# Start addresses of the float32r operand tiles: 32 and 224 bytes past a multiple of 256, or on it

## The chip, the core and the metric

The kernel runs on one core of one Trainium2 chip. The metric is the time of one execution on the device in microseconds (us). Before the change it is 1198.25 us, the median of three runs (1197.19 to 1199.11 us).

## The reference

All inputs are float32. Three layers follow one another, over 4 x 576 = 2304 tokens of width 8 heads x 64 = 512:

```
a      = softmax of phi over the tokens, per memory slot      # 32 slots a head
k_m    = a^T k ;  v_m = a^T v                                 # 32 x 64 per head
x      = softmax(q k_m^T / 8) v_m                             # 2304 x 512
h      = x @ w_in ;  g = h * clip(h + 3, 0, 6) / 6            # 512 -> 2048
x      = g @ w_out                                            # 2048 -> 512
p      = probs / (sum(probs) + 1e-9)                          # 4 experts
out    = sum over e of p[:, e] * (relu(x @ w1[e]) @ w2[e])    # 512 -> 1024 -> 512
```

## The kernel before

A large product is made of three float32r matmuls (`PASSES`): each operand is kept as a rounded part and the rest, (hi, lo) side by side in one tile, and hi x hi, hi x lo and lo x hi are summed in PSUM. The two attention products with short sums, the transposes and `u_mm` stay in plain float32; they are few.

First stage: attention and the first FFN, over four blocks of 512 of the 2048 hidden columns. `u_mm` folds a block of `w_in` into `v_m` and gives tile `u`; `g1` (line 528) multiplies a 128-column slice of `u` (stationary) with a half of the batch's attention tile `attnT` (moving, 288 tokens); line 535 to 539 and the casts at lines 287 and 290 make `g`; `g2` (line 555) multiplies slices of `w_out` (stationary) with `g` (moving, 288 wide). The order of this stage is worked out by a planner while the program is built, from fixed costs, and is then fixed.

Second stage: the four experts, 8 chunks `c` of 512 hidden columns. Tokens go in blocks `t` of 512, 512, 512, 512 and 256. `m1` (line 681) runs 12 matmuls for each of four slices `i`: stationary a 128 x 128 slice of a weight tile `w`, moving `x2[t]`, as wide as the block. ScalarE and VectorE make the hidden tile `h` (lines 685 and 686). `m2` (line 700) runs, two items later, 12 matmuls (6 for the short block): stationary a slice of `h`, moving a weight tile `w`, 512 wide. So an item is 12 matmuls of line 681 and 12 (6) of line 700, taking turns. VectorE adds each finished 128 x 512 result into `oacc` (line 711).

Memory: pools lie on two stacks in SBUF, one growing up (`side="left"`), one growing down (`side="right"`). Addresses below are bytes in a partition. The left stack begins at 16512, behind 16384 bytes of DMA descriptors and four constants at 32 bytes each. Pool `const` takes 512 (`ident`), 32 (`three`, padded), 288 (`pr`) and 96 bytes (`psm`, padded), so the next pool begins at 17440 = 68 x 256 + 32. Pools `rawp`, `w_lo`, `acc_lo` and, in the second stage, `w_hi`, `acc_hi`, `x_lo` follow in multiples of 256: all weight tiles `w` (float32r) and `x2[0]` lie 32 bytes past a multiple of 256. The right stack begins at 229344 = 895 x 256 + 224 and also goes in multiples of 256 down to `u`, `attnT`, `g`, and in the second stage `h` and `x2[1]` to `x2[4]`: all of these lie 224 bytes past a multiple of 256.

Slices keep this, except halves of 288 float32 = 1152 bytes = 4.5 x 256: the second half of a batch's tokens in `attnT` and the lo part of `g` begin 128 bytes further, at 96 past a multiple of 256.

| matmul | moving, bytes past a multiple of 256 | stationary |
|---|---|---|
| `g1`, line 528, 768 times, 288 wide | 224 (u = 0) or 96 (u = 1) | 224 |
| `g2`, line 555, 1536 times, 288 wide | 224 (hi, two of three) or 96 (lo) | 32 |
| `m1`, line 681, 384 times, t = 0 | 32 | 32 |
| `m1`, 1152 times, t = 1 to 3 | 224 | 32 |
| `m1`, 384 times, t = 4, 256 wide | 224 | 32 |
| `m2`, line 700, 1728 times, 512 wide | 32 | 224 |

Of the kernel before, what the change touches and what calls it, by code (L numbers as in the profile page):

```python
# [9 lines left out]
F32 = mybir.dt.float32  # L10
# [13 lines left out]
P = 128  # L24
# [101 lines left out]
def body(ctx: ExitStack, tc: tile.TileContext, phiT, kv, qT, w_in, w_out, w1, w2, dp, out):  # L126
    nc = tc.nc
    ctx.enter_context(tc.manual_schedule())

    const = ctx.enter_context(tc.tile_pool(name="const", bufs=1, side="left"))  # L130
    rawp = ctx.enter_context(tc.tile_pool(name="rawp", bufs=4, side="left"))
    w_lo = ctx.enter_context(tc.tile_pool(name="w_lo", bufs=1, side="left"))
    acc_lo = ctx.enter_context(tc.tile_pool(name="acc_lo", bufs=1, side="left"))
    ps_acc = ctx.enter_context(tc.tile_pool(name="ps_acc", bufs=1, space=PSUM))
    ps_w = ctx.enter_context(tc.tile_pool(name="ps_w", bufs=4, space=PSUM))
    ph1 = ExitStack()
    keep = ph1.enter_context(tc.tile_pool(name="keep", bufs=1, side="right"))
    wip = ph1.enter_context(tc.tile_pool(name="wip", bufs=8, side="right"))
# [618 lines left out]
```

## Time and profile before

| | |
|---|---|
| median of three runs | 1198.25 us |
| the profiled execution | 1200.89 us |
| its span in the profile | 1198.9 us |
| busy: TensorE / VectorE / ScalarE | 1175.5 / 550.9 / 329.8 us |
| granted TensorE clock, mean | 0.992 of 2.4 GHz |

The profile is of one execution. "PE" is TensorE's matmuls, "PEld" its weight loads, which run beside them; DVE is VectorE and ACT is ScalarE. The profiler gives a matmul a length that overlaps the next one's, since matmuls are pipelined. So the cost of a matmul in a stream is not its "mean ns" but the step from its start to the start of the next one. In a timeline, which merges neighbours of one line into a row, that is the start of the next row less the start of this row, divided by this row's count. Starts are given to 0.01 us.

### The profile page before, as it was taken

How to read it: one execution, taken by the hardware profiler on the slowest of the kernel's cores; microseconds unless marked ns; L12 is line 12 of the kernel's file. 1: busy time of each engine (PE TensorE's matmuls, PEld its weight loads, DVE VectorE, ACT ScalarE, POOL GpSimd, SP SyncE). 2: the span in 40 equal slices, each digit the busy share in tenths (PEclk: the TensorE clock that was granted, in tenths of full speed). 3: DMA queues.
4: the chain of work that ended last, by engine and by line, in shares of the span. 5: the costliest groups of instructions: out<-in, count | busy, mean ns of one | idle time of the engine just before them, and what ended most of it. 6: DMA issues, size and time to landing. Idle time of an engine off the chain costs nothing.

```text
span 1198.9 us, 16170 instructions
## 1 busy us (share of the span) xinstructions
PE 1175.5 (98%) x6776; PEld 1009.0 (84%) x6776; DVE 550.9 (46%) x1117; ACT 329.8 (28%) x713; POOL 1.2 (0%) x8
## 2 busy tenths in 40 slices
PE   4899999999999999999999999999999999999998
PEld 3699999999999888888888888888888888888887
DVE  7988898995665352323232323232323232323222
ACT  2665655454544231111111011011112111101100
POOL 0000000000000000000000000000000000000000
PEclk8899999999999999999999999999999999999999
DMA  9852131210100000000010010000001001000011
GB/s 358 264 172 79 39 103 37 71 54 19 36 1 1 9 18 9 27 27 18 9 36 27 1 36 27 9 27 27 18 10 36 27 1 36 27 9 1 36 55 69
DMA packets 20408, 55.86 MB, mean 47 GB/s; under 512 B 2416, under 2 KB 2416, under 8 KB 19824
## 3 DMA queue, kind: packets, MB, share of 16 engines
q1 hardware_dynamic: 20336, 54.83, 13.8%
q8 instruction: 53, 0.87, 0.3%
q14 instruction: 19, 0.16, 0.0%
HBM read 50.11 MB, written 4.72 MB: 46 GB/s over the span
## 4 chain that ended last, share of the span: by engine, by line
PE 97%; DVE 1%; ACT 1%; DMA 0%; issue 0%; ACTq 0%
PE ph L681 33%; PE pacc L700 33%; PE pacc L555 17%; PE ph L528 8%; PE psc L376 2%; PE pu L512 1%; PE pk L350 1%; PE pa L333 0%; PE pe L421 0%; DMA raw<-in_w_in 0%; ACT phi L317 0%; ACT a L340 0%; DVE oacc L711 0%; DVE w L221 0%; DVE mx L308 0%
## 5 line engine op out<-in xcount | busy, mean ns | idle before, releaser
L681 PE MATMUL ph<-x,w 128*128 128x512 f32 (+1 forms) x1920 | 426.8, 371 | 0.0
L700 PE MATMUL pacc<-w,h 128*128 128x512 f32 x1728 | 425.1, 394 | 0.0
L681 PEld LDWEIGHTS ph<-x,w 128*128 128x128 f32 x1920 | 337.9, 188 | 69.8
L700 PEld LDWEIGHTS pacc<-w,h 128*128 128x128 f32 x1728 | 322.7, 188 | 72.3
L686 DVE SCALAR_TENSOR_TENSOR h<-ph,h 128x512 fp32r<-128x512 f32 (+1 forms) x160 | 102.2, 639 | 557.2 <-ACT h L685 557.2
L685 ACT ACTIVATE h<-ph 128x512 fp32r<-128x512 f32 (+1 forms) x160 | 88.9, 555 | 673.8 <-PE ph L681 673.8
L555 PE MATMUL pacc<-g,w 128*128 128x288 f32 x1536 | 221.4, 296 | 1.7 <-DVE w L193 1.0
L555 PEld LDWEIGHTS pacc<-g,w 128*128 128x128 f32 x1536 | 208.2, 188 | 10.3 <-issue 6.7
L528 PE MATMUL ph<-attnT,u 128*128 128x288 f32 x768 | 116.8, 296 | 0.4 <-ACT vmT L365 0.4
L528 PEld LDWEIGHTS ph<-attnT,u 128*128 128x128 f32 x768 | 106.3, 188 | 5.0 <-issue 1.0
L711 DVE SCALAR_TENSOR_TENSOR oacc<-pacc,pr,oacc 128x512 f32<-128x512 f32 x126 | 86.3, 744 | 2.6 <-PE pacc L700 2.6
L287 ACT CAST g<-t 128x288 fp32r<-128x288 f32 x128 | 55.4, 434 | 89.5 <-PE pacc L555 76.8
L535 ACT ACTIVATE t<-ph,three 128x288 f32<-128x288 f32 x128 | 62.6, 501 | 32.0 <-DVE g L290 22.5
L290 DVE TENSOR_TENSOR g<-t,g 128x288 fp32r<-128x288 f32 x128 | 56.6, 454 | 23.7 <-ACT g L287 23.3
L539 DVE SCALAR_TENSOR_TENSOR t<-t,ph 128x288 f32<-128x288 f32 x128 | 56.6, 450 | 10.1 <-ACT t L535 10.1
L567 DVE TENSOR_TENSOR acc<-pacc,acc 128x288 f32<-128x288 f32 x96 | 39.7, 457 | 31.1 <-PE pacc L555 31.1
L193 DVE TENSOR_TENSOR w<-raw,w 128x512 fp32r<-128x512 f32 x64 | 43.6, 682 | 0.1
L189 ACT CAST w<-raw 128x512 fp32r<-128x512 f32 x64 | 39.1, 613 | 0.0
L376 PEld LDWEIGHTS psc<-kmT,q 128*128 128x128 f32 (+1 forms) x160 | 20.7, 213 | 3.5 <-issue 3.0
L376 PE MATMUL psc<-kmT,q 128*128 128x64 f32 (+1 forms) x160 | 21.7, 298 | 1.5 <-DVE mx L311 1.5
L333 PE MATMUL pa<-ident,phi 128*128 128x128 f32 (+1 forms) x40 | 8.4, 353 | 14.8 <-ACT phi L317 14.8
L290 DVE TENSOR_TENSOR u<-pu,u 128x512 fp32r<-128x512 f32 x32 | 21.4, 681 | 1.5 <-ACT u L287 1.5
(59 smaller groups left out, 364.2 us busy)
## 6 DMA issues: line engine op xcount, KB each, us to landing
raw<-in_w SPq DMA_DIRECT2D x64, 256.0 KB, 2.7
raw<-in_w_in SPq DMA_DIRECT2D x16, 512.0 KB, 4.0
kv<-in_kv SPq DMA_DIRECT2D x16, 512.0 KB, 7.5
raw<-in_w_out SPq DMA_DIRECT2D x16, 512.0 KB, 3.3
q<-in_qT SPq DMA_DIRECT2D x4, 1152.0 KB, 5.4
out_y<-oacc SPq DMA_DIRECT2D x18, 256.0 KB, 2.1
phi<-in_phiT SPq DMA_DIRECT2D x4, 576.0 KB, 7.9
kv<-in_kv SPq DMA_DIRECT2D x4, 256.0 KB, 9.6
```

Of the source, the lines that this page charges most:

```text
L287: nc.scalar.copy(hi, src)
L290: nc.vector.tensor_tensor(out=lo, in0=src, in1=hi.bitcast(F32), op=ALU.subtract)
L376: nc.tensor.matmul(ps[:n, j].rearrange("p (o g) m -> p g o m", o=2)[:, hp], st["q", b][:, hp, s0:s0 + n], kmT[b % 2][:, hp].rearrange("p ( ...
L528: nc.tensor.matmul(ps, uts[c, b][:, x, hq, i * P:(i + 1) * P], attnT[b][:, y, hq, u * UN:(u + 1) * UN], start=(k == 0), stop=(k == 5))
L535: nc.scalar.activation(t, st["ph", n], AF.Relu, bias=three, scale=1.0)
L539: nc.vector.scalar_tensor_tensor(out=t, in0=t, scalar=6.0, in1=st.pop(("ph", n)), op0=ALU.min, op1=ALU.mult)
L555: nc.tensor.matmul(pacc[j][:, 0:UN], w[:, x, j * P:(j + 1) * P], g[:, y], start=(i == 0 and k == 0), stop=(i == NI - 1 and k == 2))
L681: nc.tensor.matmul(ps[:, 0:T], wsp[c, kt][:, x, i * P:(i + 1) * P], x2[t][:, y, kt], start=(k == 0), stop=(k == 11))
L685: nc.scalar.activation(h[:, 0, 0:T], ps[:, 0:T], AF.Relu)
L686: nc.vector.scalar_tensor_tensor(out=h[:, 1, 0:T], in0=ps[:, 0:T], scalar=0.0, in1=h[:, 0, 0:T].bitcast(F32), op0=ALU.max, op1=ALU.subtract)
L700: nc.tensor.matmul(ps, h[:, x, j * P:(j + 1) * P], wsp[c, 4 + i][:, y], start=(i == 0 and k == 0), stop=(i == NI - 1 and k == 2))
L711: nc.vector.scalar_tensor_tensor(out=o, in0=ps, scalar=sc, in1=o, op0=ALU.mult, op1=ALU.add)
```

## The change

A tile of 56 float32 (224 bytes) a partition is put at the beginning of the left stack and another at the beginning of the right stack. Nothing reads or writes them. Everything on the left stack moves up by 224 bytes and everything on the right moves down by 224 bytes. The weight tiles and `x2[0]` come to 32 + 224 = 256, and `u`, `attnT`, `g`, `h` and `x2[1]` to `x2[4]` to 224 - 224 = 0: all begin on a multiple of 256. The 1152-byte halves (`attnT` for u = 1, the lo part of `g`) begin at 128 past one. No instruction is added, removed or moved.

```diff
     const = ctx.enter_context(tc.tile_pool(name="const", bufs=1, side="left"))
+
+    const.tile([P, 56], F32, name="edge")
     rawp = ctx.enter_context(tc.tile_pool(name="rawp", bufs=4, side="left"))
...
     ps_w = ctx.enter_context(tc.tile_pool(name="ps_w", bufs=4, space=PSUM))
+    edge = ctx.enter_context(tc.tile_pool(name="edge", bufs=1, side="right"))
+    edge.tile([P, 56], F32, name="edge_r")
     ph1 = ExitStack()
```

## Rows read from the trace of the kernel before

**Rows 1.** The page, parts 1 and 2: busy times, and the granted clock in 40 slices

```profile
PE 1175.5 (98%) x6776; PEld 1009.0 (84%) x6776; DVE 550.9 (46%) x1117; ACT 329.8 (28%) x713; POOL 1.2 (0%) x8
...
PEclk8899999999999999999999999999999999999999
```

**Rows 2.** The page, part 4: the chain that ended last, by line

```profile
PE ph L681 33%; PE pacc L700 33%; PE pacc L555 17%; PE ph L528 8%; PE psc L376 2%; PE pu L512 1%; PE pk L350 1%; PE pa L333 0%; PE pe L421 0%; DMA raw<-in_w_in 0%; ACT phi L317 0%; ACT a L340 0%; DVE oacc L711 0%; DVE w L221 0%; DVE mx L308 0%
```

**Rows 3.** Busy time by stretch; PE, PEld, DVE, ACT, POOL, granted clock, DMA share, GB/s

```profile
40.00:60.00 20.00, 18.02 (x238) 14.77 (x231) 19.15 (x48) 15.21 (x39) 0.00 (x0) 0.99 0.86 279
60.00:345.00 285.00, 284.90 (x2322) 269.68 (x2322) 232.89 (x539) 154.71 (x348) 0.00 (x0) 1.00 0.20 64
345.00:1190.00 845.00, 845.00 (x4006) 702.58 (x4005) 266.93 (x463) 145.16 (x296) 0.00 (x0) 1.00 0.07 22
```

**Rows 4.** Groups by line, who waits; count, busy us, mean ns, idle before and releaser

```profile
L681 PEld LDWEIGHTS ph<-x,w 128*128 128x128 f32 x1920 | 337.9, 188 | 69.8
...
L686 DVE SCALAR_TENSOR_TENSOR h<-ph,h 128x512 fp32r<-128x512 f32 (+1 forms) x160 | 102.2, 639 | 557.2 <-ACT h L685 557.2
L685 ACT ACTIVATE h<-ph 128x512 fp32r<-128x512 f32 (+1 forms) x160 | 88.9, 555 | 673.8 <-PE ph L681 673.8
```

**Rows 5.** Groups by line and shape, matmuls from 400 to 1100 us

```profile
L700 PE MATMUL pacc<-w,h 128*128 128x512 f32 x1511 | 372.0, 394 | 0.0
L681 PE MATMUL ph<-x,w 128*128 128x512 f32 x1345 | 329.7, 393 | 0.0
L681 PE MATMUL ph<-x,w 128*128 128x256 f32 x336 | 44.2, 281 | 0.0
```

**Rows 6.** Timeline of PE, end of block t=4, begin of t=0: start, length, line, count

```profile
489.05 1.58 PE L681 MATMUL ph<-x,w 128*128 128x256 f32 x12
490.47 1.56 PE L700 MATMUL pacc<-w,h 128*128 128x512 f32 x6
491.86 2.88 PE L681 MATMUL ph<-x,w 128*128 128x512 f32 x12
494.58 1.54 PE L700 MATMUL pacc<-w,h 128*128 128x512 f32 x6
```

**Rows 7.** Timeline of PE, end of block t=0, then t=1, in the same chunk

```profile
505.51 2.88 PE L681 MATMUL ph<-x,w 128*128 128x512 f32 x12
508.23 2.91 PE L700 MATMUL pacc<-w,h 128*128 128x512 f32 x12
510.98 2.96 PE L681 MATMUL ph<-x,w 128*128 128x512 f32 x12
513.78 2.96 PE L700 MATMUL pacc<-w,h 128*128 128x512 f32 x12
516.58 2.96 PE L681 MATMUL ph<-x,w 128*128 128x512 f32 x12
519.38 2.93 PE L700 MATMUL pacc<-w,h 128*128 128x512 f32 x12
522.14 2.96 PE L681 MATMUL ph<-x,w 128*128 128x512 f32 x12
```

**Rows 8.** Timeline of PE in the first stage, 288 wide

```profile
223.11 1.75 PE L528 MATMUL ph<-attnT,u 128*128 128x288 f32 x12
224.70 1.75 PE L555 MATMUL pacc<-g,w 128*128 128x288 f32 x12
...
231.45 0.95 PE L528 MATMUL ph<-attnT,u 128*128 128x288 f32 x6
232.24 0.95 PE L555 MATMUL pacc<-g,w 128*128 128x288 f32 x6
...
237.79 0.97 PE L528 MATMUL ph<-attnT,u 128*128 128x288 f32 x6
238.60 3.34 PE L555 MATMUL pacc<-g,w 128*128 128x288 f32 x24
241.78 0.97 PE L528 MATMUL ph<-attnT,u 128*128 128x288 f32 x6
```

## The prediction

> **What bounds the kernel now.** I read the page's busy times first: TensorE's matmuls take 1175.5 us of the 1198.9 us span, and the granted clock is at its upper level of 2.4 GHz but for the first two slices [rows 1]. The chain of waits says the same from the other end: lines 681, 700, 555 and 528, the four float32r products, hold 33 + 33 + 17 + 8 = 91% of the path [rows 2]. By stretches TensorE has no gap that counts from 60 us on: 284.9 of 285 us and 845 of 845 us [rows 3]. VectorE and ScalarE wait for it in the second stage, ScalarE 674 us ahead of line 685 and VectorE 557 us ahead of line 686, and the weight loads of line 681 have 69.8 us of idle time of their own [rows 4]. So the time is a number of matmuls times the step from one start to the next. No instruction comes or goes; only that step can change, by the operands' addresses. What the trace can say of that is whether matmuls of one shape at different addresses have different steps now.
>
> **They do.** Line 681 runs the same 12 matmuls, 512 wide, from the same weight tiles for token blocks 0 to 3. For block 0, where both operands lie 32 past a multiple of 256, a run of 12 takes 505.51 to 508.23, so 2.72 us or 226.7 ns each; the run at 491.86 to 494.58 takes the same 2.72 us [rows 6, 7]. For block 1, with `x2` at 224, the runs at 510.98 and 516.58 take 2.80 us, 233.3 ns each [rows 7]. That is 6.6 ns or 2.9% between two runs a few microseconds apart, same line, same width, same clock. Line 700, moving operand at 32 and stationary at 224, lies between: 2.75, 2.80 and 2.76 us, so 229.2, 233.3 and 230.0 ns [rows 7].
>
> **The change, part by part.** The two added tiles are written by nobody, so they cost no instruction. DMAs keep their sizes, their order and their queue, and the order on every engine is fixed when the program is built. Nothing waits anew. What moves is start addresses, and the terms are the four products.
>
> 512 wide (line 700, 1728 times; line 681 for four blocks, 1536 times; 3264 in all). From 400 to 1100 us TensorE is never idle, and the stretch holds 336 matmuls 256 wide and 1511 + 1345 = 2856 that are 512 wide [rows 5]. A 256-wide one takes (490.47 - 489.05) / 12 = 118.3 ns [rows 6], together 39.8 us, which leaves 660.2 us / 2856 = 231.2 ns for a 512-wide one. After the change both operands of all of them begin on a multiple of 256. The nearest row for that is block 0 of line 681, both operands at the same place past a multiple of 256, at 226.7 ns. I take this value: 3264 x 4.5 ns = 14.7 us less. The ends: 512 columns at the granted 2.4 GHz are 213.3 ns, and if the step fell to that, it would be 3264 x 17.9 = 58.4 us less; if all went to the dearest step that the rows show for this width, 233.3 ns, 3264 x 2.1 = 6.9 us more.
>
> 256 wide (line 681, block 4, 384 times). Now 118.3 ns with operands at 224 and 32. No row shows this width aligned. If the aligned step went with the width it would be 226.7 / 2 = 113.3 ns, 1.9 us less; if it got worse as the dearest 288-wide row does against its usual one (135.0 against 132.5), 0.8 us more. A fixed part of the step may well not shrink, so I take half of the gain, 0.9 us less.
>
> 288 wide (lines 528 and 555, 2304 times). The runs are 132.5 ns (223.11 to 224.70, and 238.60 to 241.78), 131.7 (231.45) and 135.0 (237.79) [rows 8]. Line 528 has its operands at 224 and 224 or at 96 and 224, line 555 at 224 or 96 and 32. After it half of line 528 and two thirds of line 555 are at 0 and 0, the rest at 128 and 0, since a half of 1152 bytes is no multiple of 256. The steps here don't fall apart by address as those of line 681 do, which speaks for a small effect. Ends: 226.7 x 288 / 512 = 127.5 ns would be 2304 x 5.0 = 11.5 us less; 135.0 for all would be 2304 x 2.5 = 5.8 us more. I take 131.5, by the row at 131.7 which is nearest: 2.3 us less. Some of these matmuls lie in the first 60 us, where TensorE also waits for others; a part of 2.3 us doesn't matter there.
>
> Everything else (float32 products, transposes, VectorE, ScalarE, the DMAs) also moves by 224 bytes. Their float32 matmuls have 2 + 1 + 1 = 4% of the chain [rows 2], 48 us, and a 1% change of all of them would be 0.5 us to either side; I take nothing. That TensorE stays the bound is safe: a second stage that is 15 us shorter still leaves VectorE 267 us of work in some 830 [rows 3].
>
> Sum: 14.7 + 0.9 + 2.3 = 17.9 us less. The profiled execution took 1200.9 us, so it would come to 1183.0. That execution lies 2.6 us over the median of 1198.25, so the median comes to 1180.4; I say 1180.
>
> A rule that speaks against the change: the Trainium skill, "SBUF — State Buffer", section "Specifications (TRN2)", gives SBUF lines of 16 bytes and a penalty for each step to a new line, and its section "Operand start alignment" asks of a start address no more than a multiple of the element size (and says that its runs timed nothing). Since 32 and 224 are multiples of 16 as 256 is, by that rule no step would change and the time would stay at 1198. The rows differ from it: 226.7 against 233.3 ns for two starts that both are multiples of 16 [rows 7].
>
> **The rivals.** *No effect.* Block 0 differs from blocks 1 to 3 in more than the address: in it ScalarE and VectorE also convert weights, and `x2[0]` was made in the first stage. If something of that kind sets the step, the time stays at 1198. Against it: more work beside TensorE should not make its matmuls faster, and line 700 is at 229.2 ns in the same block, so it isn't the moment. This is also what the skill's rule on lines of 16 bytes gives. Chance 0.07.
>
> *The moving operand alone decides.* Line 700's moving operand lies at 32 already, as that of the fast runs of line 681 does, and it still needs 229 to 233 ns. If it does so for a reason of its own (it alternates between the hi and lo part of one weight tile, and loads the same stationary slice twice), only blocks 1 to 3 of line 681 gain: 1152 x 6.6 = 7.6 us, 1190.6. Against it: its stationary operand at 224 is the one thing that the table of addresses gives for it. Chance 0.10.
>
> *32 is not the floor.* Nothing in the trace begins at 0. If a start at 32 costs the 512-wide step as much over one at 0 as 224 costs over 32, 6.6 ns, the step is 220.1 and 3264 x 6.6 = 21.5 us more go, to 1159; the narrower ones could add to that. For it: 226.7 is still 13.4 ns over 512 columns at 2.4 GHz. Against it: the 256-wide step is 11.6 ns over its 106.7, so most of that seems a fixed part. Chance 0.12. The Trainium skill, "TensorE: Matmul & The Clock Gate", section "Back-to-back issue gap", gives width / 2.4 + 2.5 ns for an isolated step, 215.8 at 512; an estimate by that page for all three widths is 3264 x 15.4 + 384 x 9.1 + 2304 x 10.0 = 77 us less, 1121. No row here comes near it.
>
> *Slower.* With every operand on a multiple of 256, a weight load and the moving read beside it begin on the same place within 256 bytes. If that is where they get in each other's way, the 512-wide step goes to 233.3 and, with the 128-byte halves, the 288-wide one to 135.0: 6.9 + 5.8 = 12.7 us more, 1211. It decides once the common place costs more than 4.5 ns a matmul against what the rows at 32 show. Against it: block 0 of line 681 has just that, both at 32, and is the fastest. Chance 0.04.
>
> **How the numbers follow.** My forecast has 0.67. All of it, the moving-operand rival and the rival of a lower floor are faster by over 0.2% (2.4 us, about what a measurement here can tell from no change): 0.67 + 0.10 + 0.12 = 0.89; within it 0.07; slower 0.04. The range goes from 1157 (the lower floor for 512 wide, which leaves out its further half, 0.06) to 1196 (which holds the moving-operand case and leaves out no effect and slower, 0.11): 0.17 left out. Within it, the 288-wide bounds alone move the forecast from 1171 to 1189.
>
> **What would show it.** In the timeline after, runs of 12 of line 681 last 2.72 us in all blocks 0 to 3, and those of line 700 too; the second stage is some 15 us shorter and the first some 2. If line 700 stays at 2.75 to 2.80 the moving operand alone decides; if block 0 also gets shorter than 2.72, 32 was not the floor; if blocks 1 to 3 stay at 2.80, the address was not the reason. A run of line 528 over 0.81 us for 6 would show that the 128-byte halves cost. The forecast fails if no row of line 681 gets faster, or if one that was at 226.7 gets slower.

## The result, and the profile after

The changed kernel takes 1186.38 us, the median of four runs (1184.58 to 1189.32), against 1197.72 us before: ratio 0.991, 95% interval 0.9883 to 0.9936. It is 11 us faster; 1180 was forecast. In a second series of runs, further down, the ratio was 0.9866 (0.9846 to 0.9887). Part of that spread is the clock that an execution was granted: at a mean clock of 0.993 the executions on record took 1200.5 to 1201.5 us before (four) and 1187.0 to 1187.7 after (three), at 0.997 they took 1196.7 to 1198.7 (three) and 1182.2 to 1183.1 (two). At an equal clock the change is thus worth some 14 us.

Part 5 of the page before, and then parts 1 and 5 of the page after (line 681 is now 685, line 700 is 704, 528 is 532 and 555 is 559):

```profile
L681 PE MATMUL ph<-x,w 128*128 128x512 f32 (+1 forms) x1920 | 426.8, 371 | 0.0
L700 PE MATMUL pacc<-w,h 128*128 128x512 f32 x1728 | 425.1, 394 | 0.0
```

```profile
PE 1162.9 (98%) x6776; PEld 1010.3 (85%) x6776; DVE 550.9 (46%) x1117; ACT 329.7 (28%) x713; POOL 1.2 (0%) x8
...
L685 PE MATMUL ph<-x,w 128*128 128x512 f32 (+1 forms) x1920 | 419.7, 368 | 0.0
L704 PE MATMUL pacc<-w,h 128*128 128x512 f32 x1728 | 418.3, 390 | 0.0
...
L532 PE MATMUL ph<-attnT,u 128*128 128x288 f32 x768 | 116.8, 296 | 0.4 <-ACT vmT L369 0.4
```

Counts and the other engines' busy times are as in [rows 1]. The two groups of the second stage are shorter; line 528 had 116.8 us before, as line 532 has now. The timeline of TensorE around the end of block 4 and into blocks 0 and 1, which answers to [rows 6, 7]; columns: start, length, line, count:

```profile
478.46 1.60 PE L685 MATMUL ph<-x,w 128*128 128x256 f32 x12
479.89 2.91 PE L704 MATMUL pacc<-w,h 128*128 128x512 f32 x12
482.64 1.60 PE L685 MATMUL ph<-x,w 128*128 128x256 f32 x12
...
506.06 2.88 PE L685 MATMUL ph<-x,w 128*128 128x512 f32 x12
508.78 2.88 PE L704 MATMUL pacc<-w,h 128*128 128x512 f32 x12
511.50 2.88 PE L685 MATMUL ph<-x,w 128*128 128x512 f32 x12
514.22 2.88 PE L704 MATMUL pacc<-w,h 128*128 128x512 f32 x12
516.94 2.88 PE L685 MATMUL ph<-x,w 128*128 128x512 f32 x12
```

In blocks 0 and 1 every run of 12 that is 512 wide now starts 2.72 us ahead of the next one, 226.7 ns a matmul, on line 685 and on line 704; behind a 256-wide run line 704 takes 2.75 (479.89 to 482.64). Before it was 2.72 in block 0, 2.80 in block 1 and 2.75 to 2.80 on line 700 [rows 7]. The 256-wide run got longer: 1.43 us, 119 ns, where it was 1.42 [rows 6]. The first stage, answering to [rows 8]:

```profile
225.05 1.76 PE L532 MATMUL ph<-attnT,u 128*128 128x288 f32 x12
226.64 1.75 PE L559 MATMUL pacc<-g,w 128*128 128x288 f32 x12
```

12 matmuls of line 532 in 1.59 us are 132.5 ns, the same as before to the 0.01 us of the rows.

The trace keeps the starts to the nanosecond, so the steps can be summed over all matmuls of a kind. Before and after, in us: line 681 with 512 columns 355.8 and 348.2; line 700 399.2 and 392.4; line 681 with 256 columns 45.2 and 45.8; line 528 104.3 and 104.5; line 555 208.2 and 208.6. Together that is 13.2 us less, of which the span shows 11.6. The other 1.6 us went in the first 60 us: the matmul that began at 60.05 us before begins 1.7 us later after the change. That stretch by busy time, before and then after (columns as in [rows 3]):

```profile
0.00:60.00 60.00, 40.45 (x428) 32.71 (x429) 49.17 (x114) 29.58 (x70) 1.21 (x8) 0.86 0.88 311
```

```profile
0.00:60.00 60.00, 39.44 (x403) 31.64 (x403) 49.13 (x114) 29.31 (x68) 1.20 (x8) 0.83 0.86 308
```

TensorE got 0.83 of its clock there against 0.86, and was 25 matmuls behind at 60 us. The clock varies from run to run of one kernel: the four runs of the changed kernel had mean clocks of 0.991, 0.993, 0.996 and 0.995 with times of 1189.3, 1187.0, 1185.8 and 1184.6 us.

### The profile page after: what moved, and what is told of

Its sections match the earlier page's. It is cut to its first block, busy times and chain, and to the rows that moved or that the text cites. A ratio compares the mean times of both kernels' runs of the same rounds, so it can differ in the third digit from the quotient of the medians.

```text
span 1187.3 us, 16170 instructions
## 1 busy us (share of the span) xinstructions
PE 1162.9 (98%) x6776; PEld 1010.3 (85%) x6776; DVE 550.9 (46%) x1117; ACT 329.7 (28%) x713; POOL 1.2 (0%) x8
## 4 chain that ended last, share of the span: by engine, by line
PE 97%; DVE 1%; ACT 1%; DMA 0%; issue 0%; SPq 0%; ACTq 0%
PE ph L685 33%; PE pacc L704 33%; PE pacc L559 17%; PE ph L532 9%; PE psc L380 2%; PE pu L516 1%; PE pk L354 1%; PE pa L337 0%; DMA raw<-in_w_in 0%; PE pe L425 0%; ACT phi L321 0%; ACT a L344 0%; DVE oacc L715 0%; DVE w L225 0%; DVE mx L312 0%
## 5 line engine op out<-in xcount | busy, mean ns | idle before, releaser
L685 PE MATMUL ph<-x,w 128*128 128x512 f32 (+1 forms) x1920 | 419.7, 368 | 0.0
L704 PE MATMUL pacc<-w,h 128*128 128x512 f32 x1728 | 418.3, 390 | 0.0
L559 PEld LDWEIGHTS pacc<-g,w 128*128 128x128 f32 x1536 | 208.6, 188 | 10.3 <-issue 6.7
L532 PE MATMUL ph<-attnT,u 128*128 128x288 f32 x768 | 116.8, 296 | 0.4 <-ACT vmT L369 0.4
```

Source lines behind the costliest of these rows:

```text
L532: nc.tensor.matmul(ps, uts[c, b][:, x, hq, i * P:(i + 1) * P], attnT[b][:, y, hq, u * UN:(u + 1) * UN], start=(k == 0), stop=(k == 5))
L559: nc.tensor.matmul(pacc[j][:, 0:UN], w[:, x, j * P:(j + 1) * P], g[:, y], start=(i == 0 and k == 0), stop=(i == NI - 1 and k == 2))
L685: nc.tensor.matmul(ps[:, 0:T], wsp[c, kt][:, x, i * P:(i + 1) * P], x2[t][:, y, kt], start=(k == 0), stop=(k == 11))
L704: nc.tensor.matmul(ps, h[:, x, j * P:(j + 1) * P], wsp[c, 4 + i][:, y], start=(i == 0 and k == 0), stop=(i == NI - 1 and k == 2))
```

## The experiments

Two theories stood at first. S, "same place": only the distance between the start of the moving and of the stationary operand, modulo 256, sets the step. M, "multiple of 256": each operand costs for itself, by its own start. A distance below is the start of the moving operand less that of the stationary one, modulo 256. All kernels compute the full result unless said otherwise, and have the second stage's lines a few numbers away from 681 and 700 (named in the rows).

**All at 224.** The changed kernel with another padding on the left and none on the right:

```diff
-    const.tile([P, 56], F32, name="edge")
+    const.tile([P, 48], F32, name="edge")
...
-    edge = ctx.enter_context(tc.tile_pool(name="edge", bufs=1, side="right"))
-    edge.tile([P, 56], F32, name="edge_r")
```

Expected: 

> All float32r operand tiles at 224 past a multiple of 256 (padding of 192 bytes on the left stack, none on the right). Theory S (same place: only the distance between the moving and the stationary operand's start, modulo 256, sets the step): all 512-wide matmuls at 226.7 ns as after the change, 12 of line 681's in 2.72 us in every block, about 1186 us. Theory M (multiple of 256: each operand costs for itself, and 224 is dear): block 0 rises from 2.72 to 2.80 us, the others stay, line 700 at 2.75 or more; 1198 to 1202 us.

Measured: 1186.26 us, ratio 0.9887 (0.9867 to 0.9907). TensorE's timeline, block 0 and then block 1:

```profile
501.48 2.88 PE L683 MATMUL ph<-x,w 128*128 128x512 f32 x12
504.20 2.88 PE L702 MATMUL pacc<-w,h 128*128 128x512 f32 x12
...
512.36 2.88 PE L683 MATMUL ph<-x,w 128*128 128x512 f32 x12
515.08 2.88 PE L702 MATMUL pacc<-w,h 128*128 128x512 f32 x12
```

All 2.72 us. No operand tile lies on a multiple of 256, and the whole gain is there. M is out. Worked out from the pools' sizes, `x2[1]` lies at 155616 and the last weight tile of `w_lo` at 58592 here, 256 apart modulo 512, as all of `x2[1]` to `x2[4]` and the weight tiles are. So a common place modulo 512 isn't needed.

**One padding alone.** The two added pieces, each without the other:

```diff
     # left_only
-    edge = ctx.enter_context(tc.tile_pool(name="edge", bufs=1, side="right"))
-    edge.tile([P, 56], F32, name="edge_r")
...
     # right_only
-    const.tile([P, 56], F32, name="edge")
```

Expected of the left one: 

> Only the padding of the left stack: weight tiles and x2[0] at 0, everything on the right at 224. Theory M: blocks 1 to 3 keep 2.80 us for 12 (moving operand still at 224) and line 700 keeps 2.75 to 2.80 (stationary still at 224): about 1197 us, nearly no gain. Theory S: blocks 1 to 3 are 32 apart (224 against 0), line 700 32 apart the other way; no row has that distance, so between 2.72 and 2.83 us, but block 0 stays at 2.72, and the time is that of right_only within 0.3%.

Expected of the right one: 

> Only the padding of the right stack: weight tiles and x2[0] at 32, everything on the right at 0. Theory M: 0 and 32 are both cheap (block 0 before, at 32, had 226.7 ns), so all 512-wide matmuls at 226.7 ns and about 1186 us, 11 us faster than left_only. Theory S: 32 apart as in left_only, the same time as left_only within 0.3%.

Measured: 1205.9 us (ratio 1.0032, 1.0015 to 1.005) and 1205.86 us (1.004, 1.0025 to 1.0056). Each half of the change makes the kernel slower than before; together they make it 1% faster. In M's forecast the right one would have been as fast as the whole change. The timelines, left one first, in blocks 0 and 1:

```profile
501.88 2.89 PE L683 MATMUL ph<-x,w 128*128 128x512 f32 x12
504.61 2.95 PE L702 MATMUL pacc<-w,h 128*128 128x512 f32 x12
507.40 2.96 PE L683 MATMUL ph<-x,w 128*128 128x512 f32 x12
510.20 2.96 PE L702 MATMUL pacc<-w,h 128*128 128x512 f32 x12
513.00 2.96 PE L683 MATMUL ph<-x,w 128*128 128x512 f32 x12
```

```profile
507.00 2.89 PE L684 MATMUL ph<-x,w 128*128 128x512 f32 x12
509.73 2.95 PE L703 MATMUL pacc<-w,h 128*128 128x512 f32 x12
512.52 2.96 PE L684 MATMUL ph<-x,w 128*128 128x512 f32 x12
515.32 2.96 PE L703 MATMUL pacc<-w,h 128*128 128x512 f32 x12
518.12 2.96 PE L684 MATMUL ph<-x,w 128*128 128x512 f32 x12
```

The runs are the same to 0.01 us: 2.73, 2.79, 2.80 and 2.80, although the moving operand of blocks 1 to 3 lies at 224 in one kernel and at 0 in the other. What they share, line by line, is the distance: 224 for line 681 in these blocks and 32 for line 700. One thing neither theory had: block 0, with both of its own operands on the same place, takes 2.73 and not 2.72. By the starts in the trace eleven of the steps of the run shown are at 226.7 ns and the twelfth at 235. The twelfth is the one beside which the first slice of `h` is loaded, and that is at a distance of 32. This made the third theory, tested further down.

**Every distance.** Small unused tiles ahead of each of `x2[1]` to `x2[4]` and one behind them (the numbers are float32 each; the first kernel's are shown, the second has 32, 8, 8, 32, 48):

```diff
+PADS = {1: 8, 2: 8, 3: 8, 4: 8, 5: 32}
...
+            for p in (t, t + 1) if t == 4 else (t,):
+                if p in PADS:
+                    pool().tile([P, PADS[p]], F32, name=f"pad{p}")
+                if p == t:
+                    x2[t] = pool().tile([P, 2, 4, TB[t][1]], F32R, name=f"x2_{t}")
```

Expected of the first: 

> The changed kernel with small unused tiles between x2[1] to x2[4], so that the moving operand of line 681 starts at 0, 32, 64, 96 past a multiple of 256 in blocks 0 to 3, and at 128 in the 256-wide block 4, the stationary one at 0 in all. Theory S: 2.72 us for 12 in block 0, more in each of blocks 1 to 3 (2.76 to 2.82). Theory M: block 1 at 2.72 too, blocks 2 and 3 between 2.72 and 2.80. Block 4, 1.43 us for 12 after the change, moves by less than 0.05 us by either.

Expected of the second: 

> As x2_32_64_96, with the moving operand of line 681 at 0, 128, 160, 192 past a multiple of 256 in blocks 0 to 3 and at 64 in the 256-wide block 4, the stationary at 0. Same place modulo 256: blocks 1 to 3 all above 2.72 us for 12, at 2.76 to 2.82; block 3 as blocks 1 to 3 before the change (224 against 32, also 192 apart), 2.80. Same place modulo 128: block 1 (128 apart) at 2.72.

Measured: one execution each, 1198.61 and 1197.69 us. The timeline of the first in blocks 1, 2 and 3 (32, 64 and 96 apart), then of the second (128, 160 and 192):

```profile
516.11 2.97 PE L690 MATMUL ph<-x,w 128*128 128x512 f32 x12
518.91 2.92 PE L709 MATMUL pacc<-w,h 128*128 128x512 f32 x12
...
538.32 2.93 PE L690 MATMUL ph<-x,w 128*128 128x512 f32 x12
541.08 2.93 PE L709 MATMUL pacc<-w,h 128*128 128x512 f32 x12
...
560.49 2.98 PE L690 MATMUL ph<-x,w 128*128 128x512 f32 x12
563.31 2.92 PE L709 MATMUL pacc<-w,h 128*128 128x512 f32 x12
```

```profile
517.66 2.95 PE L690 MATMUL ph<-x,w 128*128 128x512 f32 x12
520.45 2.90 PE L709 MATMUL pacc<-w,h 128*128 128x512 f32 x12
...
545.32 2.97 PE L690 MATMUL ph<-x,w 128*128 128x512 f32 x12
548.12 2.90 PE L709 MATMUL pacc<-w,h 128*128 128x512 f32 x12
...
567.48 2.96 PE L690 MATMUL ph<-x,w 128*128 128x512 f32 x12
570.28 2.90 PE L709 MATMUL pacc<-w,h 128*128 128x512 f32 x12
```

So 12 matmuls of line 690 take 2.80, 2.76 and 2.82 us at a distance of 32, 64 and 96, and 2.79, 2.80 and 2.80 at 128, 160 and 192; at 224 it was 2.80 above, at 0 it is 2.72. Only distance 0 is cheap, so 128 is not the period. The kernel before fits in: its line 681 was at 192 in blocks 1 to 3 (2.80 us), and its line 700, moving at 32 and stationary at 224, at 64. Line 700 lay between, at 2.75 to 2.80 us: by the starts its steps in [rows 7] behind block 0 go round in 229, 232 and 226 ns, and those of line 690 in block 2 of the first kernel, also at 64, settle into the same round. Only multiples of 32 were tried, because tiles are laid out in steps of 32 bytes. Line 709, whose own operands are both on a multiple of 256 here, takes 2.76 us for 12 in the mean of the first kernel and 2.73 of the second, where the changed kernel has 2.72: a disturbed stretch takes a few matmuls to die away.

**h alone off.** To find which two reads meet, the changed kernel with only `h` moved to 224, by a pad behind the three `h` buffers:

```diff
         h = hpool.tile([P, 2, 512], F32R, tag="h", name="h")
+        if n == 0:
+            hpool.tile([P, 8], F32, name="hpad", bufs=1)
```

(and a pad of 56 behind `x2[4]`, which keeps `x2` where it was). Expected: 

> The changed kernel with h alone at 224 past a multiple of 256 (weight tiles and x2 at 0). Theory L (the moving read of a matmul meets the weight load of the next one, which runs beside it): in line 681 eleven of 12 steps stay at 226.7 ns and the twelfth, beside which the first slice of h is loaded, rises to about 235; in line 700 the last of 12, beside which a weight slice at 0 is loaded, falls back towards 226.7, the others at about 233. Theory O (a matmul's own two operands meet): all 12 of line 681 at 226.7, all 12 of line 700 dear. Both: 1728 x 6 ns = some 10 us over the changed kernel, about 1196 us.

Measured: one execution, 1198.1 us. The timeline as block 0 ends and block 1 begins:

```profile
508.12 2.95 PE L711 MATMUL pacc<-w,h 128*128 128x512 f32 x12
510.91 2.89 PE L690 MATMUL ph<-x,w 128*128 128x512 f32 x12
513.64 2.95 PE L711 MATMUL pacc<-w,h 128*128 128x512 f32 x12
516.43 2.89 PE L690 MATMUL ph<-x,w 128*128 128x512 f32 x12
```

Line 690 takes 2.73 us and line 711 2.79. By the starts, the runs of line 690 shown have eleven steps of 226 and 227 ns and a last one of 235; that last one is 235 in all 126 runs of blocks 0 to 3 that line 711 follows in the records. The run of line 711 at 513.64 has 233, 235, 230, 235, 234, 234, 231, 235, 233, 234, 231 and a last one of 227. The last step falls back like this in 127 of the 157 runs of line 711 in the records; the other 30, all at the 256-wide block, end on some 233. The last step of line 690 belongs to a matmul whose own operands are both on a multiple of 256, while `h` is being loaded for the next (both the twelfth matmul and that load start at 513.41); the last step of line 711 to a matmul with a stationary operand at 224, while a weight slice at 0 is loaded. So what counts is the moving operand of a matmul against the stationary operand of the next one (theory L), as L forecast to the place and the size where an undisturbed stretch is broken. Where a disturbed one ends, single steps don't follow the pair so strictly, as the 30 runs show. The kernel before has the same: the last step of line 681 in its blocks 1 to 3, whose moving operand and the next `h` both lie at 224, is 231 ns in the mean and not 226.7, and that of block 0, at a distance of 64 from the next `h`, is 226 and not dearer.

**Widths.** To see what an aligned step is made of, the 10 inner ones of the 12 matmuls of line 681 were cut; the rest of the products is left out:

```diff
+CUT = {1: (384, 128), 2: (512, 64), 3: (512, 32)}   # widths: (288, 128), (256, 128), (448, 128)
...
+                N, M = CUT.get(t, (T, P)) if 0 < k < 11 else (T, P)
+                nc.tensor.matmul(ps[0:M, 0:N], wsp[c, kt][:, x, i * P:i * P + M], x2[t][:, y, kt, 0:N],
...
```

Expected: 

> The changed kernel; in line 681, the 10 inner of 12 matmuls are cut: block 1 to 384 moving columns, block 2 to 64 stationary columns, block 3 to 32 (that part of the products is left out). Fixed theory (each weight load of 128 columns costs the moving read beside it 13.3 ns, whatever the width): block 1 at 160.0 + 13.3 = 173.3 ns a matmul; blocks 2 and 3 fall with the columns loaded, to about 220.0 and 216.7 ns. Proportional theory (the moving read itself takes 17/16 of the columns): block 1 at 170.0 ns, blocks 2 and 3 stay at 226.7.

Expected of the second: 

> The changed kernel; in line 681, the 10 inner of 12 matmuls are cut to 288 moving columns in block 1, 256 in block 2 and 448 in block 3 (the rest of the products is left out). Fixed theory: 133.3, 120.0 and 200.0 ns a matmul. Proportional theory: 127.5, 113.3 and 198.3 ns.

Measured, one execution each: 1175.6 and 1117.27 us. Blocks 1 and 2 of the first, then of the second (a row is named by its first matmul's shape):

```profile
512.84 2.38 PE L687 MATMUL ph<-x,w 128*128 128x512 f32 x12
515.05 2.92 PE L706 MATMUL pacc<-w,h 128*128 128x512 f32 x12
...
533.25 2.92 PE L687 MATMUL ph<-x,w 128*128 128x512 f32 x12
536.01 2.89 PE L706 MATMUL pacc<-w,h 128*128 128x512 f32 x12
```

```profile
506.32 1.93 PE L687 MATMUL ph<-x,w 128*128 128x512 f32 x12
508.09 2.89 PE L706 MATMUL pacc<-w,h 128*128 128x512 f32 x12
...
528.61 1.81 PE L687 MATMUL ph<-x,w 128*128 128x512 f32 x12
530.26 2.90 PE L706 MATMUL pacc<-w,h 128*128 128x512 f32 x12
```

By the starts, the first of the ten cut ones steps 113 ns at 256 columns, 128 at 288, 171 at 384 and 199 at 448, as the proportional theory has it; but then it rises and settles: 120 at 256 and 173 to 174 at 384, as the fixed theory has it, between 130 and 135 at 288 and 199 and 207 at 448. The means over all of a width are 119.3, 131.3, 175.9 and 202.7 ns. In the rows, 12 of which two are whole take 2.21 us at 384, 1.77 at 288 and 1.65 at 256. Cutting the loaded columns made the 512-wide step not cheaper but dearer, 230 ns at 64 (2.76 us for 12) and 231 at 32: neither theory. A matmul with fewer stationary columns also writes fewer rows of its result, so this run can't tell which of the two made the step dearer. Each theory was right on a part; why the excess is what it is stays open.

**The lo part of g on a multiple of 256.**

```diff
-        g = gt[n] = gpool.tile([P, 2, UN], F32R, tag="g", name="g")
+        g = gt[n] = gpool.tile([P, 2, 320], F32R, tag="g", name="g")
+        g = gt[n] = g[:, :, 0:UN]
```

Expected: 

> The changed kernel with g's lo part at 1280 bytes in place of 1152, so that all three passes of g2 (288 wide) have both operands on a multiple of 256. If the step of a matmul on a common place is proportional to its width (226.7 x 288 / 512): the passes of g2 come to 127.5 ns, 7 us less in all. If the part over 2.4 GHz is a fixed 13.3 ns a matmul (what 226.7 is over 213.3): 120.0 + 13.3 = 133.3 ns, so no gain, 42 matmuls in 5.55 to 5.60 us.

Measured: one execution, 1185.64 us. By the starts, without the steps over 145 ns that hold a wait or another product, line 555's step goes from 132.7 ns in the changed kernel to 131.7 (it was 132.4 in the kernel before); all its steps together fall from 208.6 to 207.1 us. Not 127.5, and not quite 133.3: at 288 columns even a common place leaves 11 to 12 ns over 288 cycles at 2.4 GHz, which are 120.0 ns.

**Both small ends together.** The last with a pad that puts the 256-wide `x2[4]` at 192, where it was faster before:

```diff
+PADS = {4: 48, 5: 16}
```

Expected: 

> The changed kernel with g's lo part at 1280 bytes and the 256-wide x2[4] at 192 past a multiple of 256. From the steps of g_1280 and of the kernel before: 1536 x 0.9 ns + 384 x 1.6 ns = 2.0 us less than the changed kernel, some 0.2%, which 5 rounds can just about tell; if what x2[4] does to line 700's steps behind it costs as much, no difference.

Expected of the changed kernel beside it: 

> The changed kernel once more, beside combo on the same chip: ratio 0.99 to the kernel before.

Measured: 1184.3 us, ratio 0.987 (0.9853 to 0.9886), and 1184.29 us, ratio 0.9866 (0.9846 to 0.9887): no difference by the medians. But the executions of this kernel had the lower clocks: at 0.993 it took 1183.8 to 1184.5 us (three), the changed kernel 1187.3 and 1187.7. In the trace the difference is there too:

```profile
474.41 1.58 PE L691 MATMUL ph<-x,w 128*128 128x256 f32 x12
475.83 2.88 PE L710 MATMUL pacc<-w,h 128*128 128x512 f32 x12
478.55 1.58 PE L691 MATMUL ph<-x,w 128*128 128x256 f32 x12
```

The 256-wide run is at 1.42 us as before the change, and line 710 behind it at 2.72 where the changed kernel has 2.75 (479.89 to 482.64). By the summed starts the three kinds of matmul are 3.0 us below the changed kernel's, which agrees with the 3.4 us at an equal clock, from few executions; over all clocks it is within the spread of the changed kernel's runs (1182.2 to 1187.7).

## Why the prediction was right, and where not

**The bound and the lever: right.** Counts and the other engines' work stayed, and the sum of TensorE's float32r steps fell by 13.2 us, where the profiled pair differs by 11.6 and executions at an equal clock by some 14.

**The 512-wide term: right.** 14.7 us was forecast, by 226.7 ns for all; the summed steps give 7.6 + 6.9 = 14.5 us, at 226.7 on line 681 and 227.2 on line 700. The missing half nanosecond is line 700 behind the 256-wide block: 2.75 for 12 instead of 2.72. What made the value good was the choice of the nearest row: both operands "at the same place past a multiple of 256" is what matters, as the run with all at 224 shows. The title's property, the multiple of 256, is only one way to have it. The forecast looked at a matmul's own two operands, though, and the pair that counts is the moving operand and the next matmul's weights. That cost nothing here, because the change puts all the 512-wide operands on one place; this part was luck.

**The 256- and 288-wide terms: this is the step that failed.** They were to give 0.9 and 2.3 us; the steps got 0.6 and 0.6 us longer. The better ends came from scaling 226.7 ns with the width (113.3 and 127.5). The runs with cut widths show such a value only for the first narrow matmul after a wide one; in a stream it is 120 and 131, so a good part of the 13.3 ns over the 213.3 of 512 cycles comes with each matmul and not with each column. The prediction named this for the 256-wide ones ("a fixed part of the step may well not shrink") and took half the gain all the same. For the 288-wide ones it took the row at 131.7, 0.79 us for 6 matmuls; starts to 0.01 us leave such a row open by up to 1.7 ns a matmul, more than the 1.0 ns that was forecast. It also counted line 528 in, whose distances the change does not touch: 0 for u = 0 and 128 for u = 1, before and after. By the starts, waits left out, its steps were 131.8 and 133.2 ns and are 131.9 and 133.6. So the 288-wide steps did differ by address before, by 1.4 ns, which the rows were too coarse to show. Line 555 went from distances of 192 and 64 to 0 and 128, and from 132.4 to 132.7 ns; only the run that has all three passes at 0 gains, 1 ns. The 256-wide step on a common place, 119.4, is even dearer than at distance 192, 117.8. With 14.5 in place of 14.7, and 1.2 us more in place of 3.2 less, the 17.9 us become some 13; the rest to the 11.6 of the profiled pair is the clock in the first 60 us. Of the 6 us by which 1180 was too low, these two terms are thus some 4.

**The rivals.** *No effect* is out by the result: blocks 1 to 3 fell to the 2.72 us of block 0. *The moving operand alone* is out: line 700 gained 6.9 us, though by this rival its moving operand was cheap before, and with `h` alone moved to 224 its steps go from 392.4 back up to 401.8 us. *32 is not the floor* is out: 226.7 ns at 0, at 32 and at 224, whenever both agree. *Slower* had the right pair of reads, a weight load and the moving read beside it, and the wrong sign: the common place is where they do not cost. Its price turned up in the halves of the change: line 700 came to 232.9 ns in both of them, and the time to 0.3 and 0.4% over before.

**Lines of 16 bytes, and two read ports.** The line of 16 bytes (the Trainium skill, "SBUF — State Buffer", section "Specifications (TRN2)") would have left the time at 1198; 2.72 against 2.80 us for starts that are all multiples of 16 differ from it. The Trainium skill, "TensorE: Matmul & The Clock Gate", section "Step-by-step: what each phase is for", says that weights and the moving operand have read ports of their own, so that loading the next weights takes no read bandwidth from the running matmul. The run with `h` at 224 differs from that too: 226.7 ns became 235 for the last matmul of line 690 by nothing but where the next weights lay.

**Open.** What the two reads share, why a distance of 64 costs less (230 ns) than the others (233 to 235), why a disturbance outlasts the pair that makes it, and why fewer stationary columns cost more. Distances that are no multiple of 32 were not tried.

## What to carry to other kernels

Where TensorE is busy without a gap and matmuls are float32r, 512 wide and each has a weight load beside it, lay moving and stationary operands so that their start addresses agree modulo 256 bytes, across all tiles that meet in neighbouring matmuls. Here that took 2% off the 512-wide step in the mean (231.4 to 227.0 ns) and some 1% off the time, for two unused tiles. Check the addresses of both stacks together, since moving one of them alone made it worse. Do not scale the gain to narrower matmuls: at 288 columns it was 1 ns, and the 256-wide step got 1.6 ns longer. Compare starts in the timeline and not mean lengths to see it.

## What the runs showed of the hardware that was not expected

The matmul pays for the next one's weights: its step goes from 226.7 to 235 ns if the slice that is loaded beside it starts at a distance of 32 from its own moving operand, modulo 256. The state has a memory: after a 256-wide run, line 704 steps 233, 236, 228, 233, 231, 226 ns and only then 227, with the same operands. And two layouts at other addresses but with the same distances (the two paddings, each alone) give steps that agree to 0.02 ns in the mean (232.33 and 232.34 on line 681).
